# Attention and gated MLP on one core: loading q and k in 1 KB runs and turning them on TensorE

## The chip, the cores and the metric

The kernel runs on 1 core of one Trainium2 chip. The metric is the device time of one execution in microseconds (us). Before the change it is 301.61 us, the median of 3 runs (297.50 to 302.17).

## The reference

Eight batches of eight heads go through causal attention with a window of 64 positions; the heads are laid side by side and go through a gated MLP with a spatial matrix.

```python
# q, k, v: (8, 8, 576, 64) float32
scores = scale * np.matmul(q, k.transpose(0, 1, 3, 2))       # scale = 1/8
mask = (rel >= 0) & (rel < 64)                               # rel = query - key
attn = softmax(where(mask, scores, -1e9))
x = (attn @ v).transpose(0, 2, 1, 3).reshape(B, S, 512)
h = np.maximum(x @ w_in, 0.0)                                # (8, 576, 1024)
u, v = h[..., :512], h[..., 512:]
v_n = (v - mean(v)) / np.sqrt(var(v) + 1e-06)
v_s = w_spatial @ v_n + b_spatial                            # over the 576 positions
out = (u * v_s) @ w_out                                      # (8, 576, 512) float32
```

## The kernel before, in words

All matmuls take float16 operands. Heads are worked in pairs: stage s = 0 to 3 of a batch is heads 2s and 2s + 1 over queries 0 to 511, and stage 4, the "rest", is queries 512 to 575 of all heads.

**Loads.** `load_qk` (L68) brings one head of q or k into 32 partitions, 288 runs of 512 bytes; `load_v_pair` (L74) and `load_v_chunk` (L82) bring V in runs of 256 bytes with positions on partitions. q and k are issued from SP; V of batch 0 from ACT, of the other batches from SP. The float32 landing tiles (`NF`, `VF`) have two buffers, the cast tiles of q and k (`NH`) one. Batches 0 and 1 are loaded at the start, batch 2 after the four head pairs of batch 0, batch a + 2 at the start of batch a's turn.

**Casts and turns.** q and k are cast to float16 (`cast_qk`: batch 0 on DVE and ACT, batch 1 on DVE and POOL, later ones on POOL, 1152 columns at a time) and turned by DVE in 32 x 32 blocks of 4 byte words (`turn`, L101), so that a head has its 64 features as 32 partitions with two features in each word. V is cast on POOL. A second copy of V, shifted by 64 positions (`vs`), is made by POOL copies for batches 0 to 2 and from batch 3 on by two SBUF to SBUF transfers issued from POOL (`shift_all`, L121).

**Attention.** `att(i, s)` first emits the normalisation left over from the stage before last (`state["post"]`: N1 is Ln of the sums on ACT, N2 is Exp of that on ACT and a multiply on DVE, L312). Then come S (scores, L221: two accumulating matmuls of 32 rows per key block and head), E (Exp on ACT, L261; mask on DVE, L270) and P of the stage before (sums L284, values L294). S and P each have one PSUM tile of two banks; everything else shares four banks (`mm`). In the rest stage two more `mm` banks take part of the scores, and three Exps read them.

**MLP.** V (L336): the half of w_in that is normalised; `p` and `o` are its parts. Q (L370, L372): V of the last 64 positions, together with the last output rows of the batch before. L: layer norm (L393). U (L403): the other half. G (L423): the spatial matmul and the gate (L426). O (L442): w_out, an ACT copy (L445) and a store, from ACT's queue for batches 0 to 2 and from SP's afterwards. W (L453), once: 25 PE transposes of w_spatial, evacuated by ACT and DVE. `warm` issues matmuls on zeros that nothing reads.

**Order.** Every engine runs its instructions in the order in which the program emits them. That order is written out by hand as strings for `run(a, seq)`: letters are the units above for batch a, `A` and `T` are attention and turn of batch a + 1. After each unit one function of `state["post"]` is emitted. In batch 0 the attention of batch 1 stands behind G, with the casts and turns of each pair in front of its stage (`k_turn`). Batches 1 and 2 have their `A` from U1 on; batch 3 and later begin them after V2.

Of the kernel before, what the change touches and what calls it, by code (L numbers as in the profile page):

```python
# [13 lines left out]
B = 8  # L14
# [5 lines left out]
def kernel(  # L20
# [37 lines left out]

    def new_qkv(b):
        for x in "kq":  # L60
            NF[b, x] = inpool.tile([128, 2, 9, 2, 64], f32, tag=f"f{x}", bufs=2, name=f"f{x}{b}")
            NH[b, x] = inpool.tile([128, 2, 9, 2, 64], f16, tag=f"n{x}", bufs=1, name=f"n{x}{b}")
            TR[b, x] = apool.tile([128, 2, 576, 2], f16, tag=f"t{x}", bufs=2, name=f"t{x}{b}")
        VF[b] = inpool.tile([128, 5, 8, 64], f32, tag="vf", bufs=2, name=f"vf{b}")
        V16[b] = [inpool.tile([128, 5, 8, 64], f16, tag=f"v{y}", bufs=2, name=f"v{y}{b}")
                  for y in "ns"]

    def load_qk(b, x, h):  # L68
        g, hp = h % 4, h // 4
# [25 lines left out]
    def cast_qk(b, x, hp, copy, p0=0, p1=128):  # L95
        copy(NH[b, x][p0:p1, hp, :, :, :], NF[b, x][p0:p1, hp, :, :, :])

    def turn(b, x, hp, p0=0, p1=128):
        o = TR[b, x][p0:p1, hp, :, :].rearrange("p n e -> p (n e)").bitcast(u32)
        n = NH[b, x][p0:p1, hp, :, :, :].rearrange("p k t d -> p (k t d)").bitcast(u32)  # L100
        nc.vector.transpose(o.rearrange("p (k i t) -> p k t i", i=32, t=2),  # L101
                            n.rearrange("p (k t d) -> p k t d", t=2, d=32))
# [32 lines left out]
    new_qkv(0)  # L135
    for h in range(8):
        for x in "kq":
            load_qk(0, x, h)
    for p in range(4):
        load_v_pair(0, p, nc.scalar)  # L140
    load_v_rem(0, nc.scalar)
# [3 lines left out]
    new_qkv(1)  # L145
    for p in range(4):
        for h in (2 * p, 2 * p + 1):
            for x in "kq":
                load_qk(1, x, h)
        load_v_pair(1, p, nc.sync)  # L150
    load_v_rem(1, nc.sync)
# [105 lines left out]
    def emit_E(b, s):  # L257
# [15 lines left out]
    def slot(r):  # L273
        return 64 * (2 * (r % 2) + r // 2)

    def emit_P(b, s):
# [5 lines left out]
        with nc.named_scope(f"P{b}_{s}"):  # L282
# [3 lines left out]
            for u in range(8 if s < 4 else 4):  # L286
                c0 = 64 * u if s < 4 else slot(u)
# [188 lines left out]
    def run(a, seq):  # L476
        for t in seq.split():
# [42 lines left out]

    pairs_in(0, 0, dve_copy, act_copy)
    v_in(0, 0)
    for s in range(4):
# [15 lines left out]
    run(0, "p0003 p0103")  # L539
    for f in state["post"]:  # L540
        f()
    state["post"] = []
    att(0, 5)
    run(0, "p0203 p0303")
    for f in state["post"]:
        f()
    state["post"] = []
    run(0, "p0034 o0 p0134 o1 p0234 o2 p0334 o3 Q L U0 U1 U2")
    for s in range(4):
        cast_qk(1, "q", s // 2, pool_copy, 64 * (s % 2), 64 * (s % 2) + 64)  # L550
        v_in(1, s)
    v_in(1, 4)

    def k_turn(s):
        hp, p0 = s // 2, 64 * (s % 2)
        cast_qk(1, "k", hp, dve_copy, p0, p0 + 64)
        for x in "kq":
            turn(1, x, hp, p0, p0 + 64)
# [10 lines left out]
    for f in state["post"]:  # L569
        f()  # L570
    state["post"] = []
    run(0, "A4 p1003 p1103")
    for f in state["post"]:
        f()
    state["post"] = []
    run(0, "A5 p1203 p1303")
    for f in state["post"]:
        f()
    state["post"] = []

    def batch_in(b):
        for hp in (0, 1):
            for x in "kq":
                cast_qk(b, x, hp, pool_copy)
        for c in range(5):
            cast_v_chunk(b, c, pool_copy)
        if b < 3:
            for p in range(4):
                shift_pair(b, p, pool_copy)
            shift_rem(b, pool_copy)  # L590
# [50 lines left out]
```

## Time and profile before

| What | Value |
|---|---|
| median of 3 runs | 301.61 us |
| all runs | 301.61, 302.17, 297.50 us |
| the profiled execution | 298.35 us, of which its span (first to last instruction) is 296.6 us |
| mean granted TensorE clock | 0.885 of full speed |
| busy share of the span | PE 74%, DVE 55%, ACT 52%, POOL 29% |
| DMA | 84848 packets, 43.39 MB; 40592 packets under 512 bytes |

PE is TensorE, with PEld its weight loads; DVE, ACT, POOL and SP are VectorE, ScalarE, GpSimd and SyncE. A name with q behind it (SPq) is the engine's sequencer or the queue of transfers that it issues. Names such as fq<-in_q_dram give the tile written and what is read; L101 is a line of the kernel. The granted clock is a share of full speed. Matmuls overlap, so the duration of one is longer than the distance between two. DMA share is the mean busy share of 16 transfer engines and can pass 1 where packets overlap.

### The profile page before, as it was taken

The page shows a single profiled execution, that of the slowest core. Times are in us where ns is not written, and L with a number is a line of the kernel's source. Part 1 is how long each engine was busy: PE and PEld are TensorE (multiplying, and loading weights), DVE is VectorE, ACT ScalarE, POOL GpSimd, SP SyncE. Part 2 cuts the span into 40 slices and gives each one's busy share as a digit, 9 for nine tenths or more (in the row PEclk, how much of TensorE's full clock was granted, in tenths as well). Part 3 has the DMA queues.
Part 4 walks back from the last instruction along what each step waited for, and adds up shares of the span by engine and source line. Part 5 has one row for each costly group of instructions (what it writes and reads, how often), then busy time and mean ns, then how long its engine had stood idle before and what let it go on. Part 6 is the DMA issues. An engine that isn't in the chain of part 4 may idle for free.

```text
span 296.6 us, 7014 instructions
## 1 busy us (share of the span) xinstructions
PE 219.7 (74%) x2893; PEld 116.9 (39%) x2893; DVE 162.0 (55%) x316; ACT 153.1 (52%) x279; POOL 86.4 (29%) x120
## 2 busy tenths in 40 slices
PE   7270789845667497395973979797989788797994
PEld 2130344431432255142551436454535444454451
DVE  4372358663546655246552675576639656844660
ACT  0351566123356346445464576486559556764723
POOL 3970165300267224040250215504430470000000
PEclk9685599985559689979899799997999999989999
DMA  9999999225784940787927789689969957002104
GB/s 157 198 203 216 199 178 164 49 77 132 155 154 84 187 75 31 192 171 166 198 60 185 188 164 198 166 244 197 171 170 241 198 129 210 20 2 85 60 17 159
DMA packets 84848, 43.39 MB, mean 146 GB/s; under 512 B 40592, under 2 KB 79568, under 8 KB 84816
## 3 DMA queue, kind: packets, MB, share of 16 engines
q1 hardware_dynamic: 75072, 33.04, 56.4%
q0 software_dynamic: 3024, 5.19, 9.2%
q10 hardware_dynamic: 6720, 4.72, 6.1%
q8 instruction: 22, 0.36, 0.6%
q14 instruction: 10, 0.08, 0.1%
HBM read 32.79 MB, written 9.44 MB: 142 GB/s over the span
## 4 chain that ended last, share of the span: by engine, by line
PE 47%; DVE 21%; ACT 13%; DMA 11%; issue 4%; ACTq 2%; SPq 1%; DVEq 0%
PE ps L423 11%; PE pv L336 8%; DMA fq<-in_q_dram 6%; PE po L442 6%; PE sc L221 5%; DVE x L312 5%; DVE vn L393 5%; PE oz L284 4%; PE pu L403 3%; ACT e L261 3%; ACT zi L310 3%; PE oz L294 3%; ACT ob L445 2%; DVE e L270 2%; DVE tq L101 2%
## 5 line engine op out<-in xcount | busy, mean ns | idle before, releaser
L261 ACT ACTIVATE e<-sc 128x1024 f16<-128x1024 f32 x32 | 32.7, 1023 | 44.8 <-PE sc L221 44.0
L221 PE MATMUL sc<-tq,tk 32*64 32x128 f16 (+2 forms) x1152 | 26.9, 233 | 35.1 <-DVE tq L101 34.3
L312 DVE TENSOR_TENSOR x<-oz,zi 128x512 f16<-128x512 f32 (+1 forms) x40 | 25.2, 630 | 42.0 <-ACT zi L310 41.9
L270 DVE TENSOR_TENSOR e<-e,mask 128x1024 f16<-128x1024 f16 x32 | 25.1, 783 | 36.3 <-ACT e L261 36.1
L221 PEld LDWEIGHTS <-tk 32*64 32x64 f16 x1280 | 22.9, 115 | 50.8 <-DVE tq L101 24.1
L127 POOL CAST nk<-fk 128x1152 f16<-128x1152 f32 x12 | 14.2, 1180 | 89.1 <-DVE tk L101 60.6
L423 PE MATMUL ps<-wspT,vn 128*128 128x512 f16 (+1 forms) x160 | 38.0, 387 | 0.0
L127 POOL CAST vn<-vf 128x512 f16<-128x512 f32 (+1 forms) x40 | 25.1, 636 | 41.5 <-DMA vf<-in_v_dram 41.2
L345 DVE BATCH_NORM_STATS2 st<-vs 128x6 f32<-128x512 f16 (+1 forms) x40 | 27.1, 677 | 17.0 <-ACT vs L343 17.0
L336 PE MATMUL pv<-win,x 128*128 128x512 f16 (+1 forms) x132 | 34.8, 414 | 0.0
L445 ACT COPY ob<-po 128x512 f32<-128x512 f32 x32 | 18.8, 587 | 29.4 <-PE po L442 24.2
L442 PE MATMUL po<-wout,g 128*128 128x512 f16 x128 | 32.9, 404 | 0.0
L284 PE MATMUL oz<-e,onesK 128*64 128x512 f16 x64 | 14.9, 454 | 23.5 <-DVE x L312 23.2
L403 PE MATMUL pu<-x,win 128*128 128x512 f16 x128 | 32.2, 406 | 0.0
L343 ACT ACTIVATE vs<-pv 128x512 f16<-128x512 f32 (+1 forms) x40 | 22.7, 599 | 12.8 <-PE pv L336 10.2
L426 DVE TENSOR_TENSOR g<-ps,ru 128x512 f16<-128x512 f32 x32 | 21.8, 683 | 10.2 <-PE ps L423 10.1
L302 ACT ACTIVATE ln<-oz 128x512 f32<-128x512 f32 (+1 forms) x40 | 22.1, 552 | 9.1 <-PE oz L294 5.9
L127 POOL CAST nq<-fq 128x1152 f16<-128x1152 f32 (+1 forms) x16 | 19.7, 1231 | 23.5 <-DVE x L312 14.3
L310 ACT ACTIVATE zi<-ln 128x512 f32<-128x512 f32 (+1 forms) x40 | 23.6, 589 | 2.7 <-ACT ob L445 2.1
L284 PEld LDWEIGHTS <-onesK 128*64 128x64 f16 x80 | 6.9, 110 | 39.3 <-issue 37.8
L423 PEld LDWEIGHTS <-vn 128*128 128x128 f16 (+1 forms) x160 | 14.8, 99 | 16.8 <-issue 1.3
L336 PEld LDWEIGHTS <-x 128*128 128x128 f16 (+1 forms) x132 | 13.1, 105 | 16.6 <-issue 5.1
(68 smaller groups left out, 300.1 us busy)
## 6 DMA issues: line engine op xcount, KB each, us to landing
fk<-in_k_dram SPq DMA_DIRECT2D x64, 144.0 KB, 4.5
fq<-in_q_dram SPq DMA_DIRECT2D x64, 144.0 KB, 5.3
vf<-in_v_dram SPq DMA_DIRECT2D x24, 256.0 KB, 5.7
out_dram<-ob SPq DMA_DIRECT2D x20, 256.0 KB, 2.5
out_dram<-ob ACTq DMA_DIRECT2D x12, 256.0 KB, 2.1
vf<-in_v_dram SPq DMA_DIRECT2D x15, 128.0 KB, 6.7
vs<-vn POOLq DMA_DIRECT2D x5, 320.0 KB, 4.2
vs<-vn POOLq DMA_DIRECT2D x5, 256.0 KB, 5.7
```

The source lines that it names most:

```text
L127: nc.gpsimd.tensor_copy(o, i)
L221: return [lambda e=e: nc.tensor.matmul(out, TR[b, "k"][rows, hp, 64 * key:64 * key + 64, e], TR[b, "q"][rows, hp, q0:q1, e], start=(e == 0 ...
L261: nc.scalar.activation(e2[:, :, :], sc[0][:, :, :], AF.Exp, bias=0.0, scale=0.125)
L270: nc.vector.tensor_tensor(e2[:, :, :], e2[:, :, :], m, ALU.min)
L284: nc.tensor.matmul(oz[64 * h:64 * h + 64, 1, 0:n], onesK[:, :], e2[:, h, 0:n], start=True, stop=True)
L310: nc.scalar.activation(zinv[:, 0:n], lnz[:, 0:n], AF.Exp, bias=0.0, scale=-1.0)
L312: nc.vector.tensor_tensor(x[:, 0:n], oz[:, 0, 0:n], zinv[:, 0:n], ALU.mult)
L336: nc.tensor.matmul(PV[b, j][0:jn, :], xcol(b, r, j), w_in_sb[:, r, 512:1024], start=(r == 0), stop=(r == 3))
L345: nc.vector.bn_stats(st6[0:jn, 0:6], vs[0:jn, :])
L403: nc.tensor.matmul(pu[:, :], w_in_sb[:, r, 128 * m:128 * m + 128], X[b, r][:, :], start=(r == 0), stop=(r == 3))
L423: nc.tensor.matmul(ps[:, :], VN[b, kk][0:kn, 128 * m:128 * m + 128], wspT[kk][0:kn, 0:512], start=(kk == 0), stop=(kk == 4))
L442: nc.tensor.matmul(po[:, :], G[b, r][:, 128 * j:128 * j + 128], w_out_sb[:, r, :], start=(r == 0), stop=(r == 3))
```

## The change

For batches 0 to 3 q and k are loaded by head pair: positions 0 to 511 of two heads go to 128 partitions, four positions to a partition, as 1 KB runs (`load_four`), and positions 512 to 575 of all heads to 64 partitions as 256 byte runs (`load_rest`). All loads, V of batch 0 among them, are issued from SP, in the order k, q, V of a pair, the rests after the third pair. The casts put the four positions in front (`cast_four`), for batch 0 on DVE and ACT, for batches 1 to 3 on POOL together with V's, pair by pair. PE transposes them (`emit_T`: eight transposes a stage into one `mm` bank), and two DVE copies from PSUM put the positions back in order. Scores are then single matmuls of 64 rows (`emit_S_pe`), and the rest stage needs one PSUM tile and one Exp. Batches 4 to 7 keep their loads and turns. The shifted copy of V is made by POOL for all batches (`shift_part` for 4 to 7). The orders of batches 0 to 3 are written anew.

```diff
+    NPE = 4
...
+    def load_four(b, x, s):
+        nc.sync.dma_start(four(NF[b, x], s), SRC[x][b, 2 * s:2 * s + 2, 0:512, :].rearrange(
+            "h (p t) d -> p h (t d)", t=4))
+
+    def load_rest(b, x):
+        nc.sync.dma_start(rest(NF[b, x]), SRC[x][b, :, 512:576, :].transpose([1, 0, 2]))
+
+    def cast_four(b, x, s, copy):
+        if s < 4:
+            copy(NH[b, x][:, 512 * s:512 * s + 512].rearrange("p (t h d) -> p h t d", t=4, h=2),
+                 NF[b, x][:, 512 * s:512 * s + 512].rearrange("p (h t d) -> p h t d", t=4, h=2))
+        else:
+            copy(NH[b, x][0:64, 2048:2560], NF[b, x][0:64, 2048:2560])
+
+    def load_pairs(b):
+        new_qkv(b)
+        for s in range(4):
+            for x in "kq":
+                load_four(b, x, s)
+            load_v_pair(b, s, nc.sync)
+            if s == 2:
+                for x in "kq":
+                    load_rest(b, x)
+        load_v_rem(b, nc.sync)
...
-    def shift_all(b):
+    def shift_part(b, part, copy):
         vn, vs = V16[b]
-        nc.gpsimd.dma_start(vs[0:64, :, :, :], vn[0:64, :, :, :])
-        nc.gpsimd.dma_start(vs[64:128, 1:5, :, :], vn[64:128, 0:4, :, :])
+        c = 2 * part
+        if part < 2:
+            copy(vs[0:64, c:c + 2, :, :], vn[0:64, c:c + 2, :, :])
+            copy(vs[64:128, c + 1:c + 3, :, :], vn[64:128, c:c + 2, :, :])
+        else:
+            shift_rem(b, copy)
...
+    def emit_T(b, s):
+        tp = psp.tile([128, 1024], f16, tag="mm", bufs=4, name=f"tp{b}_{s}")
+        n = 512 if s < 4 else 256
...
+                    for t in range(4):
+                        nc.tensor.transpose(tp[:, n * y + 128 * t:n * y + 128 * t + 128],
+                                            w[:, t, :], id16[:, :])
...
+            o = TR[b, x][:, :].rearrange("p (a n) -> p a n", a=4)
+            if s < 4:
+                nc.vector.tensor_copy(o[:, s, 0:512].rearrange("p (n t) -> p t n", t=4),
+                                      tp[:, n * y:n * y + n].rearrange("p (t n) -> p t n", t=4))
...
+    def emit_S_pe(b, s):
+        sc = psp.tile([128, 2, 512], f32, tag="sc", bufs=1, name=f"sc{b}_{s}")
...
+                    for h in (0, 1):
+                        d = slice(64 * h, 64 * h + 64)
+                        nc.tensor.matmul(sc[r:r + 64, h, c0:c1], K[d, s, 64 * key:64 * key + 64],
+                                         Q[d, s, c0:c1], start=True, stop=True)
...
+    def batch_in(b):
+        if b < NPE:
+            for s in range(4):
+                pairs_in(b, s, pool_copy, pool_copy)
+                v_in(b, s)
+                if s == 2:
+                    pairs_in(b, 4, pool_copy, pool_copy)
+            v_in(b, 4)
+            return
...
         att(0, s)
-        warm(6)
-    new_qkv(2)
-    load_batch(2)
+        warm(4)
+        emit_T(0, s + 1)
+        warm(2)
+    load_pairs(2)
+    batch_in(1)
...
-    run(0, "U3 W0 W1 W2 W3 W4 U4 G0 G1 G2")
-    k_turn(0)
-    run(0, "G3 G4 A0 O0")
-    k_turn(1)
-    run(0, "A1 O1 O2")
-    k_turn(2)
-    run(0, "A2 O3")
-    k_turn(3)
-    run(0, "A3")
...
+    run(0, "W0 W1 W2 W3 W4 U4 T0 G0 G1 T1 A0 G2 G3 T2 A1 G4 O0 T3 A2 O1 O2 T4 A3 O3")
+    run(0, "A4 p1003 p1103 F A5 p1203 p1303 F")
...
         if a == 1:
-            run(a, "p0034 o0 p0134 o1 p0234 o2 p0334 o3")
+            run(a, "p0034 o0 p0134 o1 p0234 o2 p0334 o3 Q L U0 T0 U1 T1 A0 U2 U3 T2 A1 U4 G0 T3 A2 "
+                   "G1 G2 T4 A3 G3 G4 A4 O0 O1 A5 O2 O3")
+        elif a == 2:
+            run(a, "V0 T0 V1 V2 T1 A0 V3 Q T2 A1 L U0 U1 U2 T3 A2 U3 U4 G0 G1 T4 A3 G2 G3 G4 A4 "
+                   "O0 O1 O2 A5 O3")
+        elif a == 3:
+            run(a, "V0 V1 V2 T0 V3 Q L U0 U1 A0 U2 T1 U3 U4 A1 G0 G1 A2 G2 G3 A3 G4 A4 O0 O1 O2 A5 O3")
         else:
-            run(a, "T0 V0 V1 V2 A0 V3" if a > 2 else "V0 V1 V2 V3")
-        if a > 2:
-            run(a, "Q A1 L U0 T1 U1 U2 U3 A2 U4 G0 G1 A3 G2 G3 G4 A4 O0 O1 O2 A5 O3")
-        else:
-            run(a, "Q L T0 U0 U1 A0 U2 U3 U4 A1 G0 T1 G1 G2 A2 G3 G4 A3 O0 O1 A4 O2 O3 A5")
+            run(a, "T0 V0 V1 V2 A0 V3 Q A1 L U0 T1 U1 U2 U3 A2 U4 G0 G1 A3 G2 G3 G4 A4 O0 O1 O2 A5 O3")
```

`F` emits all of `state["post"]` at once.

## Rows read from the trace of the kernel before

**Rows 1.** Windows: stretch, its length, busy us per engine, clock, DMA share, GB/s.

```profile
0.00:28.50 28.50, 12.42 (x138) 5.85 (x139) 13.42 (x38) 6.68 (x7) 14.91 (x29) 0.79 1.16 193
...
45.90:60.20 14.30, 11.62 (x102) 6.48 (x102) 11.21 (x23) 4.88 (x11) 6.04 (x9) 1.00 0.65 98
60.20:89.10 28.90, 17.32 (x265) 9.57 (x265) 13.54 (x20) 11.79 (x19) 6.30 (x7) 0.59 0.59 134
89.10:126.70 37.60, 24.64 (x353) 13.81 (x350) 19.03 (x34) 18.71 (x34) 13.32 (x18) 0.90 0.53 116
126.70:163.70 37.00, 26.16 (x355) 13.99 (x354) 18.57 (x35) 18.91 (x34) 9.50 (x13) 0.92 0.75 156
163.70:192.40 28.70, 24.79 (x360) 13.08 (x356) 18.21 (x36) 17.39 (x33) 11.01 (x15) 0.94 0.85 176
192.40:220.40 28.00, 24.43 (x356) 13.46 (x354) 17.84 (x34) 17.97 (x34) 8.86 (x11) 0.94 0.90 187
```

**Rows 2.** Chain that ended last, in order of time: start, us, what.

```profile
15.16 13.31 DMA fq<-in_q_dram
...
28.50 1.15 ACT nq L133
```

**Rows 3.** Timeline of PE: start, us, line and shapes, count, idle before and releaser.

```profile
45.86 3.63 PE L403 MATMUL pu<-x,win 128*128 128x512 f16 x16
...
53.80 4.50 PE L423 MATMUL ps<-wspT,vn 128*128 128x512 f16 x20
...
60.18 0.66 PE L221 MATMUL sc<-tq,tk 32*64 32x128 f16 x32 [1.29 <-DVE tq L101]
...
100.22 1.07 PE L221 MATMUL sc<-tq,tk 32*64 32x128 f16 x32 [5.88 <-DVE tq L101]
...
117.39 0.22 PE L221 MATMUL sc<-tq,tk 32*64 32x64 f16 x2
...
138.32 0.67 PE L221 MATMUL sc<-tq,tk 32*64 32x128 f16 x32 [3.62 <-DVE tq L101]
...
167.97 0.67 PE L221 MATMUL sc<-tq,tk 32*64 32x128 f16 x32
```

**Rows 4.** Timeline of POOL (start, us), and the page's transfers of w_in.

```profile
12.41 1.66 POOL L202 DMA_DIRECT2D win<-in_moe_w_in_dram  x2
...
win<-in_moe_w_in_dram POOLq DMA_DIRECT2D x2, 512.0 KB, 10.0
```

**Rows 5.** The page's DMA queues: packets, MB, share of 16 engines.

```profile
q1 hardware_dynamic: 75072, 33.04, 56.4%
...
q10 hardware_dynamic: 6720, 4.72, 6.1%
```

**Rows 6.** Timeline of PE, the transposes of w_spatial.

```profile
50.07 1.98 PE L453 MATMUL wps<-id,wnat 128*128 128x128 f16 x20 [0.58 <-ACT ru L405]
```

**Rows 7.** Groups by form: busy us, mean ns of one, idle before and releaser.

```profile
L312 DVE TENSOR_TENSOR x<-oz,zi 128x512 f16<-128x512 f32 x32 | 21.9, 684 | 39.0 <-ACT zi L310 38.9
L127 POOL CAST vn<-vf 128x512 f16<-128x512 f32 x32 | 20.3, 637 | 40.2 <-DMA vf<-in_v_dram 40.1
...
L127 POOL COPY vs<-vn 64x512 f16<-64x512 f16 x27 | 17.7, 655 | 1.4
...
L101 DVE STREAM_TRANSPOSE tk<-nk 128x576 uint32<-128x576 uint32 x12 | 9.2, 764 | 0.0
...
L130 DVE COPY wspT<-wps 128x576 f16<-128x576 f16 x2 | 0.8, 437 | 0.0
```

**Rows 8.** Line L270 (min/median/max ns), and layer norm in the timeline of DVE.

```profile
L270 DVE TENSOR_TENSOR e<-e,mask x32: 658/693/1515, 17.4 to 265.9; 128x1024 f16<-128x1024 f16 x32
...
96.11 2.71 DVE L393 TENSOR_SCALAR vn<-vs,mv,rs 128x512 f16<-128x512 f16 x5 [0.61 <-ACT rs L385]
...
174.04 1.69 DVE L393 TENSOR_SCALAR vn<-vs,mv,rs 128x512 f16<-128x512 f16 x5
```

**Rows 9.** Waits of SP's queue: us in total, times, longest us.

```profile
SPq L84 <- DMA out_dram<-ob: 36.1, 5, 15.2
```

More of the change, by code (lines that the diff above doesn't have):

```diff
@@ L66, in new_qkv, with four, rest, pairs_in @@
                   for y in "ns"]
+    def four(t, s):
+        return t[:, 512 * s:512 * s + 512].rearrange("p (h n) -> p h n", h=2)
+    def rest(t):
+        return t[0:64, 2048:2560].rearrange("p (h d) -> p h d", h=8)
+    def load_four(b, x, s):
[19 more added lines that the diff above has]
+        load_v_rem(b, nc.sync)
+    def pairs_in(b, s, copy_k, copy_q):
+        cast_four(b, "k", s, copy_k)
+        cast_four(b, "q", s, copy_q)
+    def two(t):
+        return t[:, 0:2304].rearrange("p (a k t d) -> p a k t d", a=2, k=9, t=2)
     def load_qk(b, x, h):
@@ L71, in load_qk @@
         nc.sync.dma_start(
-            NF[b, x][32 * g:32 * g + 32, hp, :, :, :].rearrange("p k t d -> p k (t d)"), s)
+            two(NF[b, x])[32 * g:32 * g + 32, hp, :, :, :].rearrange("p k t d -> p k (t d)"), s)
     def load_v_pair(b, p, eng):
@@ L93, in load_batch, with cast_qk, turn @@
             load_v_chunk(b, c, nc.sync)
[L95 to L100, printed above, removed]
+    def cast_qk(b, x, hp, copy):
+        copy(NH[b, x][:, 1152 * hp:1152 * hp + 1152], NF[b, x][:, 1152 * hp:1152 * hp + 1152])
+    def turn(b, x, hp):
+        o = TR[b, x][:, 1152 * hp:1152 * hp + 1152].bitcast(u32)
+        n = NH[b, x][:, 1152 * hp:1152 * hp + 1152].bitcast(u32)
         nc.vector.transpose(o.rearrange("p (k i t) -> p k t i", i=32, t=2),
@@ L133, in act_copy @@
         nc.scalar.copy(o, i)
[L135 to L141, printed above, removed]
+    load_pairs(0)
     nc.scalar.add_instruction(
@@ L144 @@
                                  ins=[], outs=[]))
[L145 to L151, printed above, removed]
+    load_pairs(1)
     scratch = cpool.tile([128, 512], f16, name="scratch")
@@ new lines, in emit_S_pe @@
+    def emit_S_pe(b, s):
+        sc = psp.tile([128, 2, 512], f32, tag="sc", bufs=1, name=f"sc{b}_{s}")
+        SC[b, s] = [sc]
+        K, Q = (TR[b, x][:, :].rearrange("p (a n) -> p a n", a=4) for x in "kq")
+        with nc.named_scope(f"S{b}_{s}"):
+            if s < 4:
+                for key in range(8):
+                    r = 64 * (key % 2)
+                    c0 = 0 if key == 1 else 64 * key
+                    c1 = min(512, 64 * key + 128)
+                    for h in (0, 1):
+                        d = slice(64 * h, 64 * h + 64)
+                        nc.tensor.matmul(sc[r:r + 64, h, c0:c1], K[d, s, 64 * key:64 * key + 64],
+                                         Q[d, s, c0:c1], start=True, stop=True)
+            else:
+                for p in range(4):
+                    for key in (8, 7):
+                        r = 64 * (key % 2)
+                        for h in (0, 1):
+                            d = slice(64 * h, 64 * h + 64)
+                            nc.tensor.matmul(sc[r:r + 64, h, 64 * p:64 * p + 64],
+                                             K[d, p, 64 * key:64 * key + 64], Q[d, p, 512:576],
+                                             start=True, stop=True)
@@ L482, in run @@
             elif c == "T":
-                if a + 1 < B:
+                if a + 1 < NPE:
+                    emit_T(a + 1, n)
+                elif a + 1 < B:
                     for x in "kq":
                         turn(a + 1, x, n)
+            elif c == "F":
+                for f in state["post"]:
+                    f()
+                state["post"] = []
+            elif c == "p":
+                V_mm(a + n // 1000, n // 100 % 10, n // 10 % 10, n % 10)
+            elif c == "o":
+                V_out(a, n)
             else:
@@ L519, in v_in @@
             shift_rem(b, pool_copy)
+    def batch_in(b):
+        if b < NPE:
+            for s in range(4):
[5 more added lines that the diff above has]
+            return
+        for hp in (0, 1):
+            for x in "kq":
+                cast_qk(b, x, hp, pool_copy)
+        for c in range(5):
+            cast_v_chunk(b, c, pool_copy)
+            if c in (1, 3, 4):
+                shift_part(b, c // 2, pool_copy)
     pairs_in(0, 0, dve_copy, act_copy)
     v_in(0, 0)
+    emit_T(0, 0)
     for s in range(4):
@@ L533 @@
         att(0, s)
-        warm(6)
-    new_qkv(2)
-    load_batch(2)
+        warm(4)
[3 more added lines that the diff above has]
+    batch_in(1)
     att(0, 4)
[L539 to L542, printed above, removed]
+    run(0, "p0003 p0103 F")
     att(0, 5)
[L544 to L558, printed above, removed]
-    run(0, "U3 W0 W1 W2 W3 W4 U4 G0 G1 G2")
-    k_turn(0)
-    run(0, "G3 G4 A0 O0")
-    k_turn(1)
-    run(0, "A1 O1 O2")
-    k_turn(2)
-    run(0, "A2 O3")
-    k_turn(3)
-    run(0, "A3")
[L569 to L590, printed above, removed]
-        else:
-            shift_all(b)
+    run(0, "p0203 p0303 F p0034 o0 p0134 o1 p0234 o2 p0334 o3 Q L U0 U1 U2 U3")
+    run(0, "W0 W1 W2 W3 W4 U4 T0 G0 G1 T1 A0 G2 G3 T2 A1 G4 O0 T3 A2 O1 O2 T4 A3 O3")
+    run(0, "A4 p1003 p1103 F A5 p1203 p1303 F")
     for a in range(1, B):
```

60 lines of the change are left out of this document (34 added, 26 removed).

## The prediction

> **What bounds the kernel now.** I read the windows by stage first. I cut them where the first w_in matmuls of a batch start (89.1, 126.7, 163.7, 192.4 us), because from there each batch runs the same sequence. Three regimes show [rows 1]. From 163.7 us on a batch takes 28.7 and 28.0 us with PE busy 24 to 25 of them at a clock of 0.94: PE sets the pace. Batches 1 and 2 take 37.6 and 37.0 us for the same PE work, so some 9 us of each are waits. Before that lie 89.1 us for batch 0, with PE at 12.4 of 28.5 us and DMA full (share 1.16, 193 GB/s), and later 17.3 of 28.9 us at a clock of 0.59, that is mostly at 1.2 GHz, after gaps.
>
> The chain of waits names the first stretch: ACT casts the last q of batch 0 at 28.50, behind a transfer issued at 15.16 that took 13.31 us [rows 2]. Later, the timeline shows the scores of batch 1 starting only at 60.18, behind all of batch 0's G matmuls; attention and output of that batch then take until 89.1. In batches 1 and 2 attention starts 11.1 and 11.7 us into the batch (100.22, 138.32), against 4.3 us in batch 3 (167.97) [rows 3]. So the cost lies in when attention starts, not in what it costs.
>
> **The change, part by part.**
>
> **1. First loads.** The last q of batch 0 now has ahead of it k and q of four pairs (8 x 256 KiB), the two rests (2 x 128 KiB) and three pairs of V (768 KiB): 3.15 MB. Before, 5.5 MB moved by 28.5 us (193 GB/s [rows 1]), because V came on its own queue and w_in was issued at 12.41 [rows 4]. At 193 GB/s 3.15 MB take 16.3 us; 17.1 with the first issue at 0.8. Longer runs move more per packet. The queues' rows give 35.7 ns for a mean 440 B and 43 ns for 702 B (share x 16 x 296.6 us / packets [rows 5]), so some 23 ns plus 0.028 ns a byte: 30, 38 and 52 ns for 256, 512 and 1024 B. A batch was 4608 x 38 + 4608 x 30 ns and is 2048 x 52 + 1024 x 30 + 4608 x 30 ns, 11% less. That gives 15.3 us at best; 22.5 if 1 MB of w_in gets ahead. I take **17: 11.5 us earlier**. V now issues from SP behind k and q. POOL's casts of V, and w_in queued behind the third of them on POOL, move with it: w_in is issued near 14 instead of 12.4, lands 10 us later [rows 4], and is wanted near 29.
>
> **2. From there to U of batch 0** it took 17.4 us (28.50 to 45.86 [rows 2, 3]). ACT's cast falls from 1.15 to 0.5 us (512 of 1152 columns). Added is a turn on PE with its evacuation: 8 transposes at 0.1 us (20 in 1.98 [rows 6]) and two DVE copies from PSUM. No row shows a copy from PSUM with a strided output. The nearest are 0.437 us for 576 contiguous columns and 0.684 us for 512 columns of a two-input op reading PSUM [rows 7]; I take 0.684, since order is restored by steps of four elements. So 0.8 + 1.4 - 0.65, partly under the warm matmuls: **+1**; U at 35.4 (33 to 41).
> VectorE: DVE Perf Modes in the Trainium skill (What auto-detection actually checks) says two 16-bit elements a cycle need step 1 in every tensor; the strided output would then run at one a cycle, (512 + 150) / 0.96 = 690 ns, an estimate, and no run here shows it. By the contiguous row instead (0.39 for 512 columns) a pair would be 0.6 us shorter on DVE and the sum 1 to 2 us lower, since DVE has slack where PE sets the pace.
>
> **3. Batch 1 under batch 0's G and O.** U, W and U4 run as before: G started 7.9 us after U (53.80 [rows 3]), so T0 is near 43.3. T0, G0, G1, T1 cost 0.8 + 2.2 + 0.8 (20 G matmuls in 4.50 us), so S of batch 1 starts near **47** instead of 60.18. Data for that: batch 0, the weights (2.2 MB as f16) and batch 1, 9.3 MB, are in at 48 us by 193 GB/s; its pair 3 is wanted near 53: cover of 5 us. POOL casts all its k and q (before: k on DVE), 10 casts of 0.64 us, interleaved with V's casts and 0.655 us shifts [rows 7]: 3.2 us a pair, below the loads' pace. From S to the w_in matmuls of batch 1 took 28.9 us (60.18 to 89.1). Now G2 to G4, O0 to O3, five S and P and three T stand in it. With 1.1 us a G, 0.9 an O, 0.5 an S, 1.0 a P and 0.8 a T the six stages from A0 on are 3.6 + 3.9 + 3.9 + 3 + 3.3 + 2 = 19.7 us; the two like stretches of batches 1 and 2 took 26.4 and 25.4, with all of G and most of U in them. I take **23**: batch 1 starts at **70** instead of 89.1 (64 to 77).
>
> **4. Batch 1** keeps its start: S of batch 2 waits for statistics, layer norm and now the evacuation behind them on DVE. PE's T0 and T1 run in that idle time. At the end A5 stands before O2 and O3, which cover the last normalisation: from the rest pair's S to the next w_in matmul took 9.3 us (117.39 to 126.7 [rows 3]) and takes S and P3 1.1, ln, zi, x and an ob 2.7, P4 0.4, O2 and O3 1.9 and some 0.4 of handing over: 6.5, so 2.8 less. 37.6 becomes **35** (32 to 38).
>
> **5. Batch 2** starts attention after V2, as batch 3 did in 28.7 us. Added on PE: 3.8 us of T, less 0.2 us for each of five S (16 matmuls for 32 in 0.67 us [rows 3]). DVE: ten evacuations, 8 x 0.68 + 2 x 0.34 = 6.1 us, for four turns of 0.76 [rows 7], 3.1 more beside 18.2 of 28.7 busy. **30.5** (28.7 to 37).
>
> **6. Batch 3** starts attention after U1: later than the 28.7 us of before, earlier than batch 2's 37.0. From 37.0 the wait before T0 (3.6) and about 2.4 of the tail go: **31** (28.7 to 34).
>
> **7. Batches 4 on**, 104.2 us from 192.4, keep their sequence. POOL copies (four of double width and one, 5.7 us) take the place of two 0.5 us DMA issues. POOL's work stretches DVE: L270 ranges from 0.66 to 1.51 us, layer norm from 1.69 to 2.71 [rows 8]. If 4.7 us of POOL meet the 15% of time that L270 runs, 0.7 us a batch at most; the transfers go in exchange. **105** (103 to 107). Casts, half the score matmuls and one Exp for three in the rest pair are counted at nothing more: PE and ACT cover them in these stages.
>
> Sum: 70 + 35 + 30.5 + 31 + 105 = 271.5 of span, against 296.6. The profiled execution was 298.35, 1.75 above its span: **273**. The median shown, 301.61, is 1.1% above that execution (lowest 297.5), so 273 may read up to 276.
>
> **Rivals.**
> *Loads late again.* SP's V loads waited 36.1 us in five waits that ended with a store, the longest 15.2 [rows 9]. Loads stay tied to stores; now k and q of later pairs stand behind V on SP, and their casts behind V's on POOL. If batch 2 finds batch 3's pairs late it goes back to 37 (+6.5), or w_in lands at 34 (+5): 278 to 280. For: DMA is full until 45. Against: 5 to 15 us of cover. 16%.
> *DVE becomes the bound.* At 1.3 us an evacuation DVE has 6 us more a batch: 27 of 30 us. Batch 0 +3, the next three +4 each: 288. Against: no row of PSUM work is above 0.69 us for 512 columns. 11%.
> *It doesn't do what it says.* The last q lands near 26 because the rate falls or other traffic gets ahead, and batch 1's attention stays chained to the casts, now POOL's: 9 us of the first gain and 14 of the second go, 273 + 24 = 297. 7%.
> *Slower: PE stays at 1.2 GHz.* Place: batches 1 to 3, where T and its evacuation cut PE's runs. A batch is 24.6 us of PE at 0.90 to 0.94, 22.6 at full speed, 45 at half. Three such batches give 70 + 135 + 105 + 1.75 = 312. It decides below a clock of 0.54 in all three (41.6 us each). For: 0.59 between 60 and 89 us [rows 1]. Against: that stretch had PE idle 40% of the time; 20 transposes at 50 us ran within a stretch (45.9 to 60.2) at clock 1.00 [rows 1, 6]. 5%.
>
> **How the numbers follow.** Forecast 61%. Two per cent is about what a measurement of this kernel can tell (its three runs span 1.6%). Forecast, late loads and DVE-bound lie below 295.6: faster 0.88; same 0.07; slower 0.05. The bounds of the terms add to 257 to 293 if all fall together; the forecast's own range is 263 to 282, and with late loads and most of the DVE case 263 to 288.
>
> **What would show it.** Step 1: ACT's cast of the last q at 15 to 20 us. Step 2: U near 35. Step 3: first S of batch 1 near 47, its w_in matmuls near 70, clock above 0.8 between. Steps 4 to 6: 35, 30.5, 31 us between those matmuls. Step 7: 105 to the end. Evacuations of 0.4 or 0.7 us settle the price; above 1 us the DVE rival holds. A cast on POOL that waits for V while a T on PE waits for that POOL would prove the loads' rival. I would be wrong if the last q still lands after 24 us.

## Result and profile after

The changed kernel takes **282.06 us** (median of 4 runs, 281.80 to 285.88) against 299.71 in the same comparison (297.50 to 302.17): a ratio of 0.946, 95% interval 0.933 to 0.960. Forecast were 273 us and a range of 263 to 288. The direction held, and so did the mechanism: earlier loads, and attention of the next batch started earlier. But 9 us of the gain did not come. The profiled execution took 281.82 us, 280.1 of it span. Medians are of all executions, ratios only of those within 1.5% of their kernel's fastest; the profiles of the second, fifth, eighth and twelfth experiment are of slower ones, at a lower granted clock and some 1 to 2% longer.

The stages, each read at the start of the same matmuls as in the prediction (us; the third to last columns are lengths). The five lower rows are experiments told below.

| Kernel | last q cast | U of batch 0 | first S of batch 1 | w_in of batch 1 | batch 1 | batch 2 | batch 3 | to the end | span |
|---|---|---|---|---|---|---|---|---|---|
| before [rows 1 to 3] | 28.5 | 45.9 | 60.2 | 89.1 | 37.6 | 37.0 | 28.7 | 104.2 | 296.6 |
| forecast | 17 | 35.4 | 47 | 70 | 35 | 30.5 | 31 | 105 | 271.5 |
| **after** | 15.6 | 37.9 | 50.9 | 75.6 | 36.4 | 33.0 | 30.6 | 104.5 | 280.1 |
| contiguous copies | 15.3 | 32.5 | 44.1 | 72.8 | 35.2 | 28.7 | 28.7 | 104.4 | 269.8 |
| stepped reads, ninth experiment | 15.5 | 33.1 | 43.3 | 76.4 | 33.6 | 29.6 | 27.0 | 102.9 | 269.5 |
| transposes in two batches | 16.0 | 33.3 | 44.5 | 66.8 | 34.8 | 29.3 | 27.0 | 103.1 | 261.0 |
| no transposes | 19.5 | 37.4 | 47.7 | 72.8 | 34.9 | 32.3 | 28.8 | 104.5 | 273.3 |
| turn first | 17.1 | 35.0 | 46.0 | 69.2 | 29.5 | 29.7 | 30.8 | 103.3 | 262.5 |

In after the last two casts of q stand in one row; the second of them, of the last head pair, starts at 15.6:

```profile
15.11 1.12 ACT L177 CAST nq<-fq 64x512 f16<-64x512 f32 x2
```

Windows of after, cut where its own batches start, with the columns of [rows 1]:

```profile
0.00:28.50 28.50, 17.84 (x183) 9.12 (x184) 18.08 (x44) 10.74 (x15) 14.76 (x29) 0.88 1.09 227
50.85:75.56 24.71, 18.11 (x240) 9.82 (x238) 14.71 (x21) 11.49 (x17) 11.52 (x19) 0.81 1.10 234
75.56:111.98 36.42, 25.55 (x313) 14.12 (x310) 23.93 (x40) 18.60 (x32) 15.98 (x28) 0.92 0.63 122
111.98:145.03 33.05, 25.68 (x316) 14.23 (x314) 24.51 (x40) 17.92 (x31) 13.19 (x15) 0.96 0.66 145
145.03:175.64 30.61, 26.23 (x355) 13.92 (x354) 20.73 (x36) 18.43 (x34) 14.72 (x17) 0.90 0.12 40
```

The first loads move 227 GB/s instead of 193. The clock is 0.81 where batch 1's attention runs, against 0.59 before. What grew is DVE (the third busy column): 23.9 and 24.5 us in batches 1 and 2, against 19.0 and 18.6 before [rows 1]. The groups by form say by what:

```profile
L268 DVE COPY tq<-tp 128x512 f16<-128x512 f16 x16 | 21.4, 1337 | 0.0
L268 DVE COPY tk<-tp 128x512 f16<-128x512 f16 x16 | 20.7, 1291 | 7.2 <-PE tp L258 7.2
L271 DVE COPY tk<-tp 128x256 f16<-128x256 f16 x4 | 1.1, 282 | 0.9 <-PE tp L263 0.9
```

An evacuation takes 1.29 to 1.34 us, not the 0.684 that the forecast took from [rows 7]. The rest stage's copies, contiguous within a pair, take 0.28 us for half the columns. The page's chain of waits shows the same (share of the span; before, DMA fq<-in_q stood in it [rows 2]):

```profile
PE 47%; DVE 35%; ACT 12%; issue 4%; ACTq 1%; POOL 0%; POOLq 0%
PE ps L509 9%; PE pv L422 8%; PE po L528 8%; DVE x L398 6%; DVE tq L268 5%; DVE tk L268 5%; PE oz L370 5%; DVE vn L479 4%; DVE st L431 4%; DVE g L512 4%; PE pu L489 3%; PE oz L380 3%; DVE e L354 3%; ACT e L344 3%; ACT zi L396 2%
```

DMA has left the chain and the evacuations are a tenth of it. Where they hurt is seen at the first scores of batch 2, in the timelines of DVE and PE:

```profile
82.91 1.70 DVE L479 TENSOR_SCALAR vn<-vs,mv,rs 128x512 f16<-128x512 f16 x5 [0.61 <-ACT rs L471]
84.53 1.27 DVE L268 COPY tk<-tp 128x512 f16<-128x512 f16 x1
85.61 1.33 DVE L268 COPY tq<-tp 128x512 f16<-128x512 f16 x1
...
86.99 0.64 PE L286 MATMUL sc<-tq,tk 64*64 64x128 f16 x16 [4.96 <-DVE tq L268]
```

PE had made these transposes by 82.0. DVE came to them after layer norm and needed 2.3 us, so PE stood still for 4.96 us. Attention of batch 2 starts 11.4 us into batch 1, as before (11.1).

### The profile page after: what moved, and what is told of

Same layout as the page of the kernel before. It is cut to its first block, busy times and chain, and to the rows that moved or that the text cites. A ratio compares the mean times of both kernels' runs of the same rounds, so it can differ in the third digit from the quotient of the medians.

```text
span 280.1 us, 6696 instructions
## 1 busy us (share of the span) xinstructions
PE 223.3 (80%) x2733; PEld 118.7 (42%) x2733; DVE 178.1 (64%) x329; ACT 151.7 (54%) x272; POOL 110.1 (39%) x157
## 4 chain that ended last, share of the span: by engine, by line
PE 47%; DVE 35%; ACT 12%; issue 4%; ACTq 1%; POOL 0%; POOLq 0%
PE ps L509 9%; PE pv L422 8%; PE po L528 8%; DVE x L398 6%; DVE tq L268 5%; DVE tk L268 5%; PE oz L370 5%; DVE vn L479 4%; DVE st L431 4%; DVE g L512 4%; PE pu L489 3%; PE oz L380 3%; DVE e L354 3%; ACT e L344 3%; ACT zi L396 2%
## 5 line engine op out<-in xcount | busy, mean ns | idle before, releaser
L171 POOL CAST nk<-fk 128x512 f16<-128x512 f32 (+2 forms) x23 | 19.2, 835 | 101.8 <-PE tp L263 61.7
L171 POOL COPY vs<-vn 64x512 f16<-64x512 f16 (+1 forms) x56 | 43.5, 776 | 3.1
L509 PE MATMUL ps<-wspT,vn 128*128 128x512 f16 (+1 forms) x160 | 40.2, 401 | 0.0
L531 ACT COPY ob<-po 128x512 f32<-128x512 f32 x32 | 18.8, 586 | 34.6 <-PE po L528 34.1
L354 DVE TENSOR_TENSOR e<-e,mask 128x1024 f16<-128x1024 f16 x32 | 25.8, 806 | 15.6 <-ACT e L344 15.5
L422 PE MATMUL pv<-win,x 128*128 128x512 f16 (+1 forms) x132 | 34.9, 412 | 0.0
L528 PE MATMUL po<-wout,g 128*128 128x512 f16 x128 | 34.7, 420 | 0.0
L489 PE MATMUL pu<-x,win 128*128 128x512 f16 x128 | 30.8, 391 | 0.0
L370 PE MATMUL oz<-e,onesK 128*64 128x512 f16 x64 | 14.2, 431 | 16.1 <-DVE x L398 15.8
L268 DVE COPY tk<-tp 128x512 f16<-128x512 f16 x16 | 20.7, 1291 | 7.2 <-PE tp L258 7.2
L509 PEld LDWEIGHTS <-vn 128*128 128x128 f16 (+1 forms) x160 | 15.3, 103 | 17.7 <-issue 3.7
L268 DVE COPY tq<-tp 128x512 f16<-128x512 f16 x16 | 21.4, 1337 | 0.0
L171 POOL CAST nq<-fq 128x512 f16<-128x512 f32 (+2 forms) x23 | 18.7, 815 | 3.9 <-DMA fq<-in_q_dram 3.9
```

What stands on the lines that cost most here:

```text
L171: nc.gpsimd.tensor_copy(o, i)
L268: nc.vector.tensor_copy(o[:, s, 0:512].rearrange("p (n t) -> p t n", t=4), tp[:, n * y:n * y + n].rearrange("p (t n) -> p t n", t=4))
L354: nc.vector.tensor_tensor(e2[:, :, :], e2[:, :, :], m, ALU.min)
L370: nc.tensor.matmul(oz[64 * h:64 * h + 64, 1, 0:n], onesK[:, :], e2[:, h, 0:n], start=True, stop=True)
L422: nc.tensor.matmul(PV[b, j][0:jn, :], xcol(b, r, j), w_in_sb[:, r, 512:1024], start=(r == 0), stop=(r == 3))
L489: nc.tensor.matmul(pu[:, :], w_in_sb[:, r, 128 * m:128 * m + 128], X[b, r][:, :], start=(r == 0), stop=(r == 3))
```

## Experiments

The theory after this reading: the price of the evacuation is all of the missing 9 us, and the output's step of four 2 byte elements makes it. Rivals: PSUM reads or POOL's traffic make it, or the 9 us are loads, order or POOL's copies.

**Order not restored.**

```diff
-nc.vector.tensor_copy(o[:, s, 0:512].rearrange("p (n t) -> p t n", t=4),
-                      tp[:, n * y:n * y + n].rearrange("p (t n) -> p t n", t=4))
+nc.vector.tensor_copy(o[:, s, 0:512], tp[:, n * y:n * y + n])
```

> Left out: the order of the positions is not restored, so the scores are of permuted positions; everything else is as after the change. Theory (the 8.6 us by which the changed kernel missed the forecast are the stepped evacuations, 1.31 us each instead of the 0.68 taken, on DVE): the contiguous copies take 0.39 to 0.45 us, DVE has 28 us less work, S of batch 1 starts near 47 to 48 us, its w_in matmuls near 70, and the time falls to 269 to 275. Rival (the new order of the units, or the four shared PSUM banks, sets the pace): the copies get as cheap, but the time stays at 279 or above.

Measured: 270.89 us, ratio 0.909 (0.902 to 0.915). The copies:

```profile
L268 DVE COPY tk<-tp 128x512 f16<-128x512 f16 x16 | 6.6, 411 | 6.0 <-PE tp L258 5.9
```

Each of the 32 copies takes 0.9 us less, and the time is 11 us less. By the table 5.4 of it are there at U of batch 0, 1.2, 4.3 and 1.9 come in batches 1 to 3, and 2.7 are lost between U and batch 1, for which see the eighth experiment. The step of the output is what makes the copy dear, not PSUM or POOL. Batch 3 holds no such copy; its 1.9 us go with the granted clock there, 1.00 against 0.90.

**The step moved to the reading side.** The same elements go to the same places; the copy walks them in the order of its output.

```diff
-nc.vector.tensor_copy(o[:, s, 0:512].rearrange("p (n t) -> p t n", t=4),
-                      tp[:, n * y:n * y + n].rearrange("p (t n) -> p t n", t=4))
+nc.vector.tensor_copy(o[:, s, 0:512].rearrange("p (n t) -> p n t", t=4),
+                      tp[:, n * y:n * y + n].rearrange("p (t n) -> p n t", t=4))
```

> The same copies walked the other way: output contiguous, PSUM read with a step of 128 elements. Theory a (the write with a step of four 2-byte elements is what is slow): a copy falls to 0.55 to 0.70 us and the time to 272 to 277. Theory b (any stepped side, or the short inner run of four, costs the same): copies stay at 1.2 us or more and the time at 280 to 283.

Measured: 275.95 us, ratio 0.925 (0.918 to 0.932).

```profile
L268 DVE COPY tq<-tp 128x512 f16<-128x512 f16 x16 | 10.8, 678 | 0.0
```

Reading PSUM with a step and writing in sequence costs 0.678 us, within 1% of the 0.684 that the forecast took, and the time is 3 us from the forecast. The price in the prediction was that of the other side of the copy. It is not the whole miss, though: this profile has U at 34.5 us, 0.9 ahead of the forecast, and then takes 43.1 us from U to batch 1, where 34.6 were forecast. There ACT stands still for 9.09 us (the eighth experiment says for what):

```profile
60.58 0.63 ACT L396 ACTIVATE zi<-ln 128x512 f32<-128x512 f32 x1 [9.09 <-DMA fk<-in_k_dram]
```

**The step moved to PE.** q is copied contiguously, and the scores read it with a step (an inner run of 4 elements at a step of 128 elements).

```diff
-Q[d, s, c0:c1]
+Q[d, s, 0:512].rearrange("p (t n) -> p n t", t=4)[:, c0 // 4:c1 // 4, :]
```

> q is evacuated contiguously and its order restored where the score matmuls read it (moving operand stepped); k is evacuated as after the change. Theory (DVE time of the evacuation is what is missing, PE reads steps at no price): q's copy 0.4 us, S stays at 0.42 us for 16 matmuls, time 275 to 278, about half of what a contiguous evacuation of both would bring. Rival (PE pays for the step): S takes 0.8 us or more, and the time stays above 279.

Measured: 279.09 us, ratio 0.939 (0.933 to 0.946), between after and the second experiment. Scores by form and the first sixteen of batch 1, here and after:

```profile
L289 PE MATMUL sc<-tq,tk 64*64 64x128 f16 x192 | 19.9, 450 | 9.5 <-DVE tq L269 9.5
49.32 1.25 PE L289 MATMUL sc<-tq,tk 64*64 64x128 f16 x16
```

```profile
L286 PE MATMUL sc<-tq,tk 64*64 64x128 f16 x192 | 6.8, 225 | 16.2 <-DVE tq L268 16.2
50.85 0.42 PE L286 MATMUL sc<-tq,tk 64*64 64x128 f16 x16
```

PE's waits for tq fall from 16.2 to 9.5 us, but a score matmul doubles, and sixteen in a row take three times as long: PE is charged for the step too, as the rival in the expectation had it.

**q's evacuation on ACT**, with the stepped output.

```diff
+(nc.scalar.copy if y else nc.vector.tensor_copy)(...)
```

> q's stepped evacuation moves from DVE to ACT, k's stays. Theory (DVE is late in batches 0 to 3, ACT has room): ACT takes 0.6 to 0.7 us a copy, DVE has 21 us less, time 274 to 278. Rival (ACT's chain of Exp and Ln is as tight, or ACT pays for the step too, above 1 us): 281 or more.

Measured: 299.03 us, ratio 1.003 (0.998 to 1.008): the whole gain is gone. ACT's group:

```profile
L268 ACT COPY tq<-tp 128x512 f16<-128x512 f16 x16 | 20.7, 1295 | 36.6 <-DVE tk L268 36.6
```

ACT pays the same 1.3 us, so the price is not DVE's own. And ACT stood idle 36.6 us in front of these copies for DVE's copy of k out of the same bank, with Ln, Exp and Relu queued behind it. The Trainium skill, PSUM — Partial Sum Buffer (PSUM bank collisions raise a hardware error), says that two engines may not be in one bank and quadrant at once and that software has to order them. The wait in the row is such an order: ACT's copy waits for the semaphore that DVE's copy counts up. No run here puts k and q into two banks, so how the loss divides between this order and ACT's own price stays open.

**Only the first loads in the new order** (kernel before, 512 byte runs, V of batch 0 on SP behind each pair).

```diff
-for h in range(8): ... load_qk(0, x, h)
-for p in range(4): load_v_pair(0, p, nc.scalar)
+for p in range(4):
+    for h in (2 * p, 2 * p + 1): ... load_qk(0, x, h)
+    load_v_pair(0, p, nc.sync)
```

> The kernel before with one part alone: batch 0's loads in the new order (k, q, then V of a pair, all from SP), still in 512 byte runs, nothing else changed. Theory (the first gain comes from what stands ahead of the last q, not from the run length): the last q is cast near 17 to 19 us instead of 28.5, U of batch 0 starts near 35 to 37 instead of 45.9, and the time falls by 8 to 11 us to 288 to 292. Rival (the longer runs and larger transfers make it): the last q is cast after 23 us and the time stays above 294.

Measured: 294.83 us in the median, ratio 0.975 (0.968 to 0.982).

```profile
20.77 1.15 ACT L133 CAST nq<-fq 64x1152 f16<-64x1152 f32 x1 [3.65 <-DMA fq<-in_q_dram]
```

The last q is cast 7.7 us earlier by order alone, and U of batch 0 starts at 38.5, where after has 37.9. Both are about 2 us later than the theory had them, far from the rival's 23. The 1 KB runs bring the cast another 5.2 us forward (the same loads put it at 15.3 to 17.1 us in the other experiments), and the transposes with their dear evacuations take nearly all of that back before U.

**Only the order of units** (kernel before: batch 2 in the order of later batches, A5 ahead of O2 O3 in batch 1).

```diff
-run(a, "T0 V0 V1 V2 A0 V3" if a > 2 else "V0 V1 V2 V3")
-if a > 2:
+run(a, "T0 V0 V1 V2 A0 V3")
+if a > 1:
...
-... G0 T1 G1 G2 A2 G3 G4 A3 O0 O1 A4 O2 O3 A5
+... G0 T1 G1 G2 A2 G3 A3 G4 A4 O0 O1 A5 O2 O3
```

> The kernel before with another part alone: batch 2 runs in the order of the later batches (attention from V2 on), and batch 1 has A5 in front of O2 and O3. Theory (batches 1 and 2 lost their time to the order of the units): batch 1 takes 34 to 36 us instead of 37.6, batch 2 29 to 32 instead of 37.0, time 288 to 292. Rival (batch 3's loads come too late for an earlier attention, so the order alone brings nothing): batch 2 stays above 35 us, with PE waiting for values of V, and the time above 295.

Measured: 296.07 us, ratio 0.994 (0.989 to 1.000); batch 1 takes 37.9 and batch 2 34.8 us. The rival holds. PE in batch 2, and POOL ahead of the later of the two rows:

```profile
132.01 0.66 PE L221 MATMUL sc<-tq,tk 32*64 32x128 f16 x32 [0.72 <-DVE tq L101]
...
141.66 0.26 PE L294 MATMUL oz<-e,vs 128*64 128x64 f16 x2 [6.04 <-DMA vs<-vn]
...
134.25 1.13 POOL L127 CAST vn<-vf 64x512 f16<-64x512 f32 x1 [3.09 <-DMA vf<-in_v_dram]
135.68 0.53 POOL L123 DMA_DIRECT2D vs<-vn  x1 [0.30 <-POOL vn L127]
```

Attention starts 6.3 us earlier than in [rows 3] (132.01 for 138.32), and then the values wait 6.04 us for the SBUF to SBUF transfer of shifted V. Two things make that wait: V's last load is late, so that its last cast starts at 134.25, and only behind that cast is the transfer issued, which lands some 5 us later. The change shifts V on POOL in the same batches, part by part behind the casts. That the order pays only with it is argued: no run has the order and POOL's shift and nothing else.

**Shift by transfers again in batches 4 to 7** (changed kernel).

```diff
-if c in (1, 3, 4):
-    shift_part(b, c // 2, pool_copy)
+nc.gpsimd.dma_start(vs[0:64, :, :, :], vn[0:64, :, :, :])
+nc.gpsimd.dma_start(vs[64:128, 1:5, :, :], vn[64:128, 0:4, :, :])
```

> The changed kernel with one part undone: the shifted copy of V of batches 4 to 7 is made by two SBUF to SBUF transfers again. Theory (POOL's copies cost at most 0.7 us a batch on DVE): 280 to 283, no difference that can be told. Rival a (the copies hold POOL and DVE up): 277 to 279. Rival b (the transfers stand behind loads and P waits for them): 284 to 288.

Measured: 280.37 us, ratio 0.942 (0.935 to 0.949), not to be told from 0.946. From batch 4 to the end it takes 103.6 us (174.2 to 277.8) against 104.5.

**Stepped reads, and batch 3 in the order of later batches** (its special order left out).

> The copies of e2_read_step, and batch 3 in the order of the later batches (attention from V2 on instead of from U1 on). Theory (the late attention of batch 3 costs what its 30.5 us are above 28): batch 3 takes 28 to 29 us and the time is 273 to 275, against 275.95 for e2_read_step. Rival (batch 4's casts or loads are not there yet, so T0 or A0 blocks PE and DVE behind it): batch 3 takes 30 us or more and the time is 276 to 280.

Measured: 270.91 us, ratio 0.905 (0.900 to 0.910); batch 3 takes 28.3 us for 30.6, and the time is 2 us better than expected. This profile also shows where the 2.7 us went that the contiguous copies gained at U and lost again. ACT and its queue:

```profile
50.98 0.58 ACT L531 COPY ob<-po 128x512 f32<-128x512 f32 x1 [0.63 <-PE po L528]
56.02 0.39 ACTq L441 DMA_DIRECT2D out_dram<-ob  x1
56.46 0.63 ACT L396 ACTIVATE zi<-ln 128x512 f32<-128x512 f32 x1 [4.89 <-DMA fk<-in_k_dram]
```

The first store of batch 0 is issued only at 56.02, 4.5 us after its copy, when a load of k lands; batch 1's normalisation waits behind it on ACT, and PE for that. The trace says what ties the two together. It lists for each transfer the semaphore that is counted up at its landing. The store has semaphore 106, as does the load of batch 2's k that SP issued at 50.53, and ACT's queue waits for 106 until 55.97. After has the same pair on 106, but the load lands at 56.40 and the copy starts only at 56.53: no wait. Where the copies are cheaper, the store comes earlier and waits: 3.97 us with contiguous copies, 9.09, 4.89 and 7.69 in the second, eighth and ninth experiment. From U to batch 1 these four take 40.4 to 43.4 us, where after takes 37.7.

**The same with the shift of batches 4 to 7 by transfers.**

> The kernel with stepped PSUM reads and batch 3 in the order of later batches (270.91 us), and in batches 4 to 7 the shift of v by SBUF to SBUF transfers instead of POOL copies. If POOL's copies stretch DVE in batches 4 on, as the 1.9 us less from batch 4 to the end in the trace of the changed kernel with those transfers says (102.5 against 104.4 us): 267 to 270 us. If the transfers only collide with loads and stores, now that DVE has slack: no change, 270 to 272 us.

The 102.5 us in that expectation was misread; it is 103.6. Measured: 271.80 us, ratio 0.914 (0.909 to 0.920), no gain: to the end 102.9 us either way. Who shifts V in the late batches is of no weight.

**Transposes in batches 0 and 1 only** (stepped reads, later batches by 32-row loads and turns, batches 2 and 3 in the order of later ones).

```diff
-    NPE = 4
+    NPE = 2
...
-U0 T0 U1 T1 A0 U2 U3 T2 A1 U4 G0 T3 A2 G1 G2 T4 A3 G3 G4 A4 O0 O1 A5 O2 O3
+U0 T0 U1 A0 U2 U3 A1 U4 T1 G0 A2 G1 G2 A3 G3 G4 A4 O0 O1 A5 O2 O3
```

> Only batches 0 and 1 by 1 KB runs and PE transposes; batches 2 to 7 by 32-row loads and DVE turns; stepped PSUM reads, shift by POOL copies in all batches. Theory (in batches 2 and 3 the gain comes from the order of units and from V shifted on POOL, and the transposes only cost PE 3.8 us and DVE 3 us a batch): 264 to 270 us, batch 1 and batch 2 no longer than 36 and 30 us. Rival (the 32-row loads, in shorter runs, come too late for attention started early): the scores of batch 2 or 3 wait for casts, 275 us or more.

Measured: 269.68 us in the median against 299.27 (262.80 to 270.78, without an interval); the profile is of the fastest execution, 262.80 us, and the other five took 267.94 or more. Batch 1 takes 34.8 and batch 2 29.3 us, 1.2 longer and 0.3 shorter than with transposes (33.6 and 29.6 in the ninth experiment); the rival, late loads, does not show. From U to batch 1 it takes 33.5 us instead of 43.4: batch 2's loads are others here, the one ahead of the first store on its semaphore landed 1.6 us before the store's copy began, and ACT waits for none. Whether that holds in the other five is not shown. S of batch 2 again waits behind layer norm:

```profile
77.00 0.93 PE L302 MATMUL sc<-tq,tk 32*64 32x128 f16 x32 [4.87 <-DVE tq L141]
```

**The whole change without transposes and 1 KB runs.** Batches 0 and 1 go by `load_qk`, casts and DVE turns pair by pair, in the new order; batches 1 to 3 have the orders of the tenth experiment.

```diff
-    NPE = 4
+    NPE = 0
...
```

> Everything of the change but the PE transposes: all batches by 32-row loads and DVE turns, batches 0 and 1 pair by pair, k and q of batch 1 cast on POOL, the new order of units, V shifted on POOL. Theory (1 KB runs and all partitions are worth only what the first loads gain, some 5 us to the last q, and order and POOL copies make the rest): last q cast near 20.8 us, first w_in matmuls of batch 1 at 76 to 80, total 270 to 277 us. Rival (attention of batch 1 stays chained to the slow loads, the casts and turns): these matmuls after 84, total 283 us or more.

Measured: 275.82 us, ratio 0.921 (0.914 to 0.927). So without its transposes, and with batch 3 in the better order, the changed kernel is 2.7% faster than with them (0.921 to 0.946). Its row in the table says where its gain lies: 8.5 us up to U, 7.8 from U to batch 1, 2.7 and 4.7 in batches 1 and 2. The edits that act there are loads in the order of use; k cast on POOL and attention under G; the order and the shift on POOL. The loads' order and the units' order were tried by themselves, the others not. The last q comes 3.9 us later than after's, but U does not.

It does not follow that transposes bring nothing. The kernels that read PSUM with the step and have batch 3 in the same order are the ones to set beside this: 0.905 (eighth) and 0.914 (ninth experiment) against 0.921 (the ninth's interval overlaps with it). Closest is the tenth, which differs in batches 0 and 1 alone: 262.80 to 270.78 us against 272.49 to 280.16, in the median 6 us less. Well walked, the transposes start U 4 us earlier (33.1 and 33.3 for 37.4), and in the ninth the store's wait of 7.69 us takes that back.

**Batch 2's first turn ahead of batch 1's statistics** (on the kernel with two transposed batches).

```diff
-p0034 o0 p0134 o1 p0234 o2 p0334 o3 Q L U0 T0 U1 A0 U2 U3 A1 U4 T1 G0 A2 ...
+T0 p0034 o0 p0134 o1 p0234 o2 A0 p0334 o3 Q A1 L U0 T1 U1 U2 U3 A2 U4 G0 G1 A3 ...
```

> The kernel that transposes on PE for batches 0 and 1 only, with batch 1 in nearly the order of later batches: batch 2's first turn stands ahead of batch 1's statistics and layer norm on DVE, and its attention starts after the third w_in group. In the kernel it is made from, batch 1 is 38.0 us, PE waits 4.87 us for that turn (77.00, behind layer norm), while the casts of batch 2 are done by 60.3. If the place of the turn on DVE sets the start of attention: scores of batch 2 near 67 instead of 77, batch 1 in 32 to 35 us, total 263 to 267 us against 269.68. If something else is late there (statistics now behind the turns, V of batch 2 on POOL until 68.5): no gain, 268 to 272 us.

Measured: **259.27 us**, ratio **0.865** (0.858 to 0.873), the best version. DVE and PE:

```profile
70.48 0.77 DVE L141 STREAM_TRANSPOSE tk<-nk 128x576 uint32<-128x576 uint32 x1
71.17 0.74 DVE L141 STREAM_TRANSPOSE tq<-nq 128x576 uint32<-128x576 uint32 x1
...
77.54 1.69 DVE L479 TENSOR_SCALAR vn<-vs,mv,rs 128x512 f16<-128x512 f16 x5
```

```profile
71.96 0.66 PE L302 MATMUL sc<-tq,tk 32*64 32x128 f16 x32 [0.68 <-DVE tq L141]
```

The scores start 2.8 us into batch 1 instead of 10.2 (67 was expected, 72 it is), and the batch takes 29.5 us instead of 34.8; the 38.0 in the expectation was cut at earlier matmuls, at 63.58, and the same cut gives 32.4 now. So the wait of batch 1 was never the price of evacuation or turn alone, but its place behind statistics and layer norm on DVE, which before, the change and my forecast all kept. The edit moves the later turns and stages of batch 1 too; what each is worth was not tried.

## Why the prediction was right, and where it was short

**Step 1, first loads: right.** 15.6 us for 17, near the best bound of 15.3: no w_in got ahead. The fifth experiment splits it: order 7.7 us, runs 5.2.

**Step 2, to U: the mis-sized term.** +1 us was taken; from the last cast to U it took 22.3 us, +4.9 on 17.4. The term that failed is the evacuation, "I take 0.684, since order is restored by steps of four elements": it measured 1.29 to 1.34. At 0.678 (second experiment) the stretch is 17.7 us, 0.7 under the forecast. The rule of the Trainium skill that the prediction cited gave 690 ns for the stepped output; the trace disagrees, and has 678 ns for the stepped read. Another page of the Trainium skill is nearer: Vector Engine (DVE) Microarchitecture Reference (5.2 Measured stream behaviour on trn2) says that a port keeps its rate only for runs of at least two adjacent 4 byte words, and lists 2.50 ns a column for an output that steps 24 words at every element. By that 512 columns and its 75 ns of fixed cost are an estimate of 1.36 us, and the copies here measured 1.29 to 1.34. No run here steps 4 byte elements.

**Step 3, batch 1 under G and O: right in place, late in time.** S at 50.9 for 47: 2.5 us come with U, the rest from evacuations at 1.3 (U to S takes 13.0 us, with 0.678 a copy 10.7). From S to batch 1 24.7 us for 23. One thing the step had at nothing and after doesn't show: a store that waits for a load. With the price that was forecast it comes, 4.89 to 9.09 us in this stretch, and batch 1 starts at 73.8 to 77.6, so the right price alone would not have met 70.

**Steps 4 and 5, batches 1 and 2: the same term.** 36.4 for 35 and 33.0 for 30.5; with 0.678 a copy 35.7 and 30.2. The terms that step 5 lists add to 31.5 (28.7 and 3.8 less 1.0), so its 30.5 left out 1 us without a reason, and met 30.2 by luck.

**Step 6, batch 3: right in number**, 30.6 for 31. The same order took 28.7 us at a granted clock of 1.00 (first experiment), where after had 0.90, which the step did not price; the order of later batches gives 28.3.

**Step 7, batches 4 on: right**, 104.5 for 105; POOL's copies cost nothing that the seventh and ninth experiments can tell.

The errors add up: 2.5 at U, 3.1 more to batch 1, 1.4, 2.5, -0.4 and -0.5 are 8.6 us, 280.1 for 271.5.

**The rivals.** *DVE becomes the bound* named the price, 1.3 us, but its time of 288 did not come: it charged four batches with full price, while batch 3 holds no evacuation (the next batch turns on DVE), and DVE is busy 24 of 33 to 36 us, not all of them. *Loads late again* did not happen. SP's queue after, to set beside [rows 9] and the first line here, which is of before (L71 loads q and k there, L111 after):

```profile
SPq L71 <- DMA out_dram<-ob: 41.8, 7, 11.8
...
SPq L111 <- POOL nk L171: 19.8, 2, 16.2
SPq L111 <- DMA out_dram<-ob: 12.6, 4, 5.8
```

Loads' waits that end with a store fell from 77.9 us (V 36.1, q and k 41.8) to 12.6. Loads now wait for POOL's casts, and no load stands in the chain of waits. *It doesn't do what it says* fell with the cast at 15.6, and *PE stays at 1.2 GHz* with granted clocks of 0.81 to 0.96 in the windows of after.

## What to carry to other kernels

Price a copy by how it walks both sides: let it write in sequence and read PSUM with the step. Before new machinery is credited with a gain, take it out and keep the order that came with it: here the order, the casts and shift on POOL and the earlier loads bring 0.921 without it; the transposes cost up to 2.7% with the dear copies, and with the cheap ones, in batches 0 and 1, the medians are 2% apart in their favour. When a step gets faster, look at what it now meets: the store that had followed a load by luck stood 4 to 9 us behind it. And look at what stands ahead of the first instruction of the next stage on its engine: a turn moved past statistics and layer norm, with the stages behind it, took 5 us off one batch.

## What the runs showed of the hardware

- 512 columns of float16 from PSUM: 0.41 us in sequence, 0.678 with a stepped read, 1.29 to 1.34 with the output at a step of 8 bytes, on DVE; 1.295 on ACT.
- A score matmul whose moving operand comes in runs of 8 bytes takes 450 ns instead of 225, and sixteen in a row 1.25 us instead of 0.42.
- Loads of 1 KB runs beside V's 256 bytes moved 227 GB/s in the first 28.5 us, against 193 with 512 byte runs before and 182 with 512 byte runs in the new order (fifth experiment).
- A transfer issued from ACT stood 4.5 us because it shares its semaphore with a load from SP that had not landed (eighth experiment).
